# Wider descriptors for thirteen zero fills, and a short-DMA ending for the last one, in a decode-attention backward kernel

## The chip, the cores and the metric

One core of one Trainium2 chip. The metric is device time in microseconds (us) of one execution. Most executions of a kernel agree within 0.3%. An execution more than 1.5% above the fastest of the same kernel is called slow; verdicts use the other, fast, runs alone. "SyncE" is the engine that issues most DMAs here, "ACT" the scalar engine and "POOL" the engine whose DMAs go through the software queue. All three feed the same 16 DMA engines. A descriptor is one contiguous piece of a transfer that one engine moves; the trace records it as a packet. A semaphore is a counter that an instruction can wait for: in the traces each of the 16 engines raises it once when its part of a large DMA has landed, and that is called an increment below.

## The reference

A forward pass and its gradients: LayerNorm, an attention over the last 4,096 of 32,768 cached positions, a squared-ReLU MLP as a gate. What matters here is the shape of two of its ten outputs.

```python
# B=2, Hkv=8, Sk=32768, Dh=128, W=4096, all bfloat16
k = k_cache[:, :, Sk - W:, :]          # only the last W positions are used
v = v_cache[:, :, Sk - W:, :]
...
_out, _vjp = jax.vjp(_f, A_x, A_k_cache, A_v_cache, A_wq, A_wo, B_w1, B_b1, B_w2, B_b2)
```

The gradients of both caches (out_2 and out_3) have the caches' full size. Only 4,096 positions of each head can be other than zero. The other 28,672 positions, 7.34 MB for each of 32 (batch, head) parts, 235 MB in all, are zeros that the kernel has to write.

## The kernel before

POOL issues the zero fills of 31 of the 32 parts. The source is a tile of zero bytes that is widened to bfloat16 by the DMA, so a row of 14,336 source bytes becomes a descriptor of 28,672 bytes. Five parts (2, 4, 6, 8, 10) are cut in odd ways; these are not touched by the change.

```python
ZR = SK - W                     # 28672 rows of 256 B
ZG = 112
zt = const.tile([P, ZG * DH], mybir.dt.uint8, name="zt")
nc.vector.memset(zt[:].bitcast(F32), 0.0)

def zf(o, q, r0, nent, rows, rep=1):
    b, hk = divmod(q, HKV)
    nr = nent * rows * rep
    v = o[b, hk, r0:r0 + nr, :].rearrange("(r p g) d -> p r (g d)", p=nent, g=rows)
    st = 4 if nent < 16 else 1
    zs = zt[0:nent * st:st, 0:rows * DH].unsqueeze(1).to_broadcast([nent, rep, rows * DH])
    sw_fill.append(nc.gpsimd.dma_start(out=v, in_=zs))
    return r0 + nr
...
for qi in range(ZQ - 1):
    r = 0
    for n, rows, rep in zshort.get(qi, ((P, ZG, ZR // (P * ZG)),)):
        r = zf(*zparts[qi], r, n, rows, rep)
```

The compute chain runs beside the fills. It loads blocks of K and V (4.19 MB each), and stores their gradients. At its end SyncE stores dw2 and dw1, then issues the zeros of the 32nd part as one DMA of 512 descriptors of 14,336 B. This DMA is held back until the last fill but one has landed. ACT stores dwo last.

```python
last = nc.sync.dma_start(out=out_6.rearrange("(p k) f -> p k f", k=DK), in_=dw1_st[:])
b, hk = divmod(zparts[ZQ - 1][1], HKV)
v = out_3[b, hk, 0:ZR, :].rearrange("(r p g) d -> p r (g d)", p=P, g=ZG // 2)
zs = zt[:].bitcast(BF16).unsqueeze(1).to_broadcast([P, 2 * ZR // (P * ZG), ZG * DH // 2])
with tc.issue_after(last.ins):
    fin = nc.sync.dma_start(out=v, in_=zs)
tc.add_manual_dep(fin.ins, sw_fill[-2].ins.name, ...)
for j in range(NJ):
    ...                          # dwo, 32 matmuls and copies
dma_store.dma_start(out=out_5.rearrange("(p j) m -> p j m", j=NJ), in_=wo[:])
```

## Time and profile before

The median was 769.4 us over 6 runs (769.01 to 769.58).

| Reading | Value |
|---|---|
| span of the profiled run | 767.3 us |
| bytes moved, mean rate | 326.72 MB, 426 GB/s |
| dw2, dw1 issued | 701.4, 708.4 us |
| zeros of part 32 issued (SyncE) | 715.9 us |
| last packet of the POOL fills ends | 749.7 us |
| store of dwo issued, last data | 723.2, 748.7 us |
| last zeros of the 16 engines | 761.11 to 765.15 us |
| SyncE passes its wait for them | 765.49 us |

The ends of packets come from their records in the trace. The page of the kernel before, first its span, then the row of DMA busyness in 40 slices (9 means 90% or more), the rate in the same slices, and the queues (packets, MB, share of the 16 engines):

```profile
span 767.3 us, 9390 instructions
...
DMA  9999999999999999999999999999999999999997
GB/s 359 429 432 421 434 430 426 431 431 436 426 425 433 433 428 428 435 426 433 436 425 433 430 434 426 434 433 432 427 436 430 426 427 438 429 430 425 434 427 321
DMA packets 14202, 326.72 MB, mean 426 GB/s; under 512 B 2341, under 2 KB 2350, under 8 KB 2360
...
q0 software_dynamic: 9728, 227.55, 70.2%
q1 hardware_dynamic: 2698, 56.63, 17.8%
q10 hardware_dynamic: 1736, 41.95, 12.9%
```

The DMA engines are full from the first slice to the last but one, so the kernel can only become faster if the bytes move faster, or if the start or the end is used better. The busy shares of the other engines (PE 53%) don't matter here.

The time line of SyncE's issues after 700 us (start, duration, line, what is issued):

```profile
701.39 0.35 SPq L603 DMA_DIRECT2D out_dram<-dw_st  x1
708.37 0.35 SPq L611 DMA_DIRECT2D out_dram<-dw_st  x1
715.88 0.39 SPq L616 DMA_DIRECT2D out_dram<-zt  x1
```

POOL's waits (in total, how often, the longest):

```profile
POOL out_dram L96 <- DMA out_dram<-zt: 529.6, 30, 36.9
```

POOL waits 30 times for an earlier fill before it issues the next one. The operands of its DMAs show why: eight semaphores are used in rotation, and the issue of a DMA waits until the DMA that had its semaphore before has landed on all engines. SyncE and ACT share another eight in the same way.

The end of the kernel before, in windows. The last two columns are the busy share of the DMA engines and their rate:

```profile
core 0: us, PE busy (x) PEld busy (x) DVE busy (x) ACT busy (x) POOL busy (x), PEclk, DMA share, GB/s
758.00:761.00 3.00, 0.00 (x0) 0.00 (x0) 0.00 (x0) 0.00 (x0) 0.00 (x0) 0.50 1.03 440
...
762.00:763.00 1.00, 0.00 (x0) 0.00 (x0) 0.00 (x0) 0.00 (x0) 0.00 (x0) 0.50 0.37 158
...
764.00:765.00 1.00, 0.00 (x0) 0.00 (x0) 0.00 (x0) 0.00 (x0) 0.00 (x0) 0.50 0.07 29
...
766.00:767.00 1.00, 0.00 (x0) 0.00 (x0) 0.00 (x0) 0.00 (x0) 0.00 (x0) 0.50 0.00 0
```

From 761 us on the engines run out of work one by one: 0.07 of 16 engines is one engine. That one ends about 1 us after all the others.

### The profile page before, as it was taken

Reading aid. Unit: us, or ns where it says so; the run is one execution under the profiler, and the core shown is the slowest. Engines: PE = TensorE matmul, PEld = TensorE weight load, DVE = VectorE, ACT = ScalarE, POOL = GpSimd, SP = SyncE. Lnnn points to the kernel's source line nnn. Section 1 sums busy time; section 2 is a strip of 40 time slices with the busy share of each in tenths; the row PEclk is TensorE's granted clock in tenths of the full one; section 3 lists DMA queues with packets and bytes.
Section 4 is the critical chain, followed back from the end, with each engine's and each line's share of the span. In section 5 each row is a group of like instructions: output and inputs, shape, how many; then the busy total and the mean of one; then the engine's idle time right before and its main releaser. Section 6 shows DMA issues by size and latency. Waiting matters only on the chain.

```text
span 767.3 us, 9390 instructions
## 1 busy us (share of the span) xinstructions
PE 409.0 (53%) x4110; PEld 267.9 (35%) x4118; DVE 277.1 (36%) x484; ACT 214.8 (28%) x313; POOL 31.9 (4%) x55
## 2 busy tenths in 40 slices
PE   0166765847503757770385667304748853768600
PEld 0153464734103655430254543004635421342200
DVE  3034252455401346450152465302337541247500
ACT  0034441245500234560020255300244542004400
POOL 3000110110000010000000000000000000000000
PEclk9998898967755995775567958756986875655555
DMA  9999999999999999999999999999999999999997
GB/s 359 429 432 421 434 430 426 431 431 436 426 425 433 433 428 428 435 426 433 436 425 433 430 434 426 434 433 432 427 436 430 426 427 438 429 430 425 434 427 321
DMA packets 14202, 326.72 MB, mean 426 GB/s; under 512 B 2341, under 2 KB 2350, under 8 KB 2360
## 3 DMA queue, kind: packets, MB, share of 16 engines
q0 software_dynamic: 9728, 227.55, 70.2%
q1 hardware_dynamic: 2698, 56.63, 17.8%
q10 hardware_dynamic: 1736, 41.95, 12.9%
q8 instruction: 32, 0.52, 0.2%
q14 instruction: 8, 0.07, 0.0%
HBM read 45.62 MB, written 280.50 MB: 425 GB/s over the span
## 4 chain that ended last, share of the span: by engine, by line
DMA 36%; PE 32%; DVE 15%; ACT 8%; issue 4%; ACTq 0%; DVEq 0%; SPq 0%
DMA out_dram<-nat 15%; DMA nat<-in_A_k_cache_dram 9%; DMA nat<-in_A_v_cache_dram 8%; PE ov L403 6%; PE s_ps L376 4%; PE tp L370 4%; DMA b_bf<-in_B_b_dram 4%; DVE tT L149 3%; PE dp_ps L376 3%; DVE ds_bf L450 2%; ACT p_bf L437 2%; DVE nat L149 2%; PE wps L621 2%; ACT tT L147 2%; ACT nat L147 1%
## 5 line engine op out<-in xcount | busy, mean ns | idle before, releaser
L370 PE MATMUL tp<-pperm,nat 128*128 128x128 bf16 x1024 | 84.1, 233 | 129.0 <-DMA nat<-in_A_v_cache_dram 111.0
L149 DVE COPY tT<-tp 128x1024 bf16<-128x1024 bf16 x96 | 64.0, 688 | 202.5 <-PE tp L370 201.9
L370 PEld LDWEIGHTS <-nat 128*128 128x128 bf16 x1024 | 73.5, 105 | 135.3 <-DMA nat<-in_A_v_cache_dram 112.7
L147 ACT COPY tT<-tp 128x1024 bf16<-128x1024 bf16 x32 | 32.4, 1012 | 258.0 <-PE tp L370 258.0
L147 ACT CAST nat<-ov 128x512 bf16<-128x512 f32 x160 | 87.8, 589 | 54.0 <-PE ov L403 27.5
L149 DVE CAST nat<-ov 128x512 bf16<-128x512 f32 x96 | 65.3, 690 | 49.3 <-PE ov L403 48.1
L96 POOL DMA_DIRECT2D out_dram<-zt x47 | 30.8, 659 | 532.8 <-DMA out_dram<-zt 529.6
L403 PE MATMUL ov<-bd,ds_bf 128*128 128x512 bf16 x124 | 48.7, 467 | 6.7 <-DVE nat L149 4.0
L403 PE MATMUL ov<-bd,p_bf 128*128 128x512 bf16 x124 | 47.4, 446 | 5.3 <-DVE nat L149 1.8
L376 PE MATMUL dp_ps<-tT,zdo 128*128 128x256 bf16 x256 | 42.0, 298 | 14.6 <-DVE tT L149 8.3
L376 PE MATMUL s_ps<-tT,zq 128*128 128x256 bf16 x256 | 39.4, 279 | 13.2 <-DVE tT L149 9.5
L376 PEld LDWEIGHTS <-zdo 128*128 128x128 bf16 x256 | 25.9, 105 | 23.3 <-issue 19.7
L392 PE MATMUL ps<-t,nat 128*128 128x16 bf16 x1024 | 28.5, 173 | 7.8 <-DVE bd L360 7.8
L392 PEld LDWEIGHTS <-nat 128*128 128x128 bf16 x1024 | 28.6, 103 | 11.0 <-issue 5.8
L376 PEld LDWEIGHTS <-zq 128*128 128x128 bf16 x256 | 24.7, 99 | 19.9 <-issue 17.6
L488 PE MATMUL wps<-dq_rows,xn_bf 2*128 2x512 bf16 x32 | 14.2, 515 | 23.6 <-ACT wq L147 18.3
L384 PE MATMUL tp<-ident_bf,p_bf 128*128 128x128 bf16 x64 | 7.5, 312 | 35.0 <-ACT p_bf L437 35.0
L437 ACT ACTIVATE p_bf<-e_sb,rl 32x512 bf16<-32x512 f32 x16 | 22.8, 1424 | 3.4 <-DVE rl L434 3.2
L149 DVE CAST wq<-wps 128x512 bf16<-128x512 f32 x16 | 11.0, 690 | 31.5 <-PE wps L488 31.1
L147 ACT CAST dw_st<-wps 128x512 bf16<-128x512 f32 x15 | 8.8, 585 | 47.7 <-PE wps L601 44.9
L450 DVE SCALAR_TENSOR_TENSOR ds_bf<-dp_ps,delta,p_bf 32x512 bf16<-32x512 f32 x16 | 21.7, 1354 | 0.2
L403 PEld LDWEIGHTS <-ds_bf 128*128 128x128 bf16 x128 | 13.3, 111 | 23.1 <-issue 20.7
(196 smaller groups left out, 452.5 us busy)
## 6 DMA issues: line engine op xcount, KB each, us to landing
out_dram<-zt POOLq DMA_DIRECT2D x26, 7168.0 KB, 163.5
out_dram<-nat ACTq DMA_DIRECT2D x8, 4096.0 KB, 26.6
nat<-in_A_v_cache_dram SPq DMA_DIRECT2D x4, 4096.0 KB, 31.0
nat<-in_A_k_cache_dram SPq DMA_DIRECT2D x4, 4096.0 KB, 25.9
out_dram<-zt POOLq DMA_DIRECT2D x4, 3584.0 KB, 56.4
out_dram<-zt SPq DMA_DIRECT2D x1, 7168.0 KB
out_dram<-zt POOLq DMA_DIRECT2D x1, 5040.0 KB, 83.3
wo<-in_A_wo_dram SPq DMA_DIRECT2D x1, 4096.0 KB, 38.2
```

Of the source, the lines that this page charges most:

```text
L96: sw_fill.append(nc.gpsimd.dma_start(out=v, in_=zs))
L147: nc.scalar.copy(out=out_ap, in_=in_ap)
L149: nc.vector.tensor_copy(out=out_ap, in_=in_ap)
L370: nc.tensor.transpose(tp[:, j, :], nat[:, g * CC + half * CH + j, :], pperm[:].rearrange("p b k -> p (b k)"))
L376: nc.tensor.matmul(out_ps[:, half * CH * PB:(half + 1) * CH * PB], lhsT=zbuf[:, pr, o:o + R], rhs=tT[:, :, pr, :], start=(g == 0 and pr == ...
L384: nc.tensor.transpose(tp[:, cc, :], src[:, half * CH + cc].rearrange("r k b -> r (k b)"), ident_bf[:, :])
L392: nc.tensor.matmul(ps[:], lhsT=nat[:, g * CC + half * CH + cc, :], rhs=cols[half][:, cc, :, g, :], start=(half == 0 and g == 0 and cc == 0 ...
L403: nc.tensor.matmul(ov[:], lhsT=src[:, cc].rearrange("r k b -> r (k b)"), rhs=bd[:, gh * 4:(gh + 1) * 4, :], start=True, stop=True)
L437: nc.scalar.activation(out=p_bf[rb, :, :, pr], in_=e_sb[rb], func=ACT.Copy, scale=rl[rb, 0:1])
L450: nc.vector.scalar_tensor_tensor(out=ds_bf[rb, :, :, pr], in0=dp_c[rb], scalar=delta[rb, 0:1], in1=p_bf[rb, :, :, pr], op0=ALU.subtract, o ...
L488: nc.tensor.matmul(wps[:], lhsT=xn_bf[:, k:D:DK], rhs=dq_rows[:, :], start=True, stop=True)
L621: nc.tensor.matmul(wps[:], lhsT=o_rows[:, j:N:NJ], rhs=ds_rows[:, :], start=True, stop=True)
```

## The change

Its intent is to halve the number of descriptors where the fills have the engines to themselves (source bytes widened to 4-byte elements, 57,344 B for each descriptor), and to give the engines different amounts at the very end, so that they finish together. Of the zeros of part 32, 384 rows go into eight short DMAs over the first 2, 4, 6 to 14 and then 8 engines.

```diff
@@ def zf
-        v = o[b, hk, r0:r0 + nr, :].rearrange("(r p g) d -> p r (g d)", p=nent, g=rows)
+        v = o[b, hk, r0:r0 + nr, :]
+        w = rows * DH
+        if w > ZG * DH:
+            v = v.bitcast(F32)
+            w //= 2
+        v = v.rearrange("(r p g) d -> p r (g d)", p=nent, g=rows)
         st = 4 if nent < 16 else 1
-        zs = zt[0:nent * st:st, 0:rows * DH].unsqueeze(1).to_broadcast([nent, rep, rows * DH])
+        zs = zt[0:nent * st:st, 0:w].unsqueeze(1).to_broadcast([nent, rep, w])
@@
+    zlong = (3, 5, 7, 11, 12, 16, 17, 18, 19, 22, 23, 24, 28)
@@
-        for n, rows, rep in zshort.get(qi, ((P, ZG, ZR // (P * ZG)),)):
+        whole = (P, ZR // P, 1) if qi in zlong else (P, ZG, ZR // (P * ZG))
+        for n, rows, rep in zshort.get(qi, (whole,)):
@@ the end
-    v = out_3[b, hk, 0:ZR, :].rearrange("(r p g) d -> p r (g d)", p=P, g=ZG // 2)
-    zs = zt[:].bitcast(BF16).unsqueeze(1).to_broadcast([P, 2 * ZR // (P * ZG), ZG * DH // 2])
-    with tc.issue_after(last.ins):
-        fin = nc.sync.dma_start(out=v, in_=zs)
-    tc.add_manual_dep(fin.ins, sw_fill[-2].ins.name,
-                      mybir.DependencyInfo(mybir.DependencyClass.Sync, mybir.DependencyReason.DATA))
+    zb = zt[:].bitcast(BF16)
+    r = 0
+    for n, g, rep, st in ((P, 56, 3, 1), (P, 53, 1, 1), (2, 1, 1, 8), (4, 2, 1, 8), (6, 3, 1, 8), (8, 4, 1, 8), (10, 5, 1, 8), (12, 6, 1, 8),
+                          (14, 7, 1, 8), (8, 13, 1, 8)):
+        v = out_3[b, hk, r:r + n * g * rep, :].rearrange("(r p g) d -> p r (g d)", p=n, g=g)
+        zs = zb[0:n * st:st, 0:g * DH].unsqueeze(1).to_broadcast([n, rep, g * DH])
+        with tc.issue_after(last.ins):
+            fin = nc.sync.dma_start(out=v, in_=zs)
+        if r == 0:
+            tc.add_manual_dep(fin.ins, sw_fill[-2].ins.name,
+                              mybir.DependencyInfo(mybir.DependencyClass.Sync, mybir.DependencyReason.DATA))
+        last = fin
+        r += n * g * rep
+    assert r == ZR
```

## The prediction

> **What bounds the kernel now.** The DMA engines. The page gives 326.72 MB at a mean of 426 GB/s over a span of 767.3 us, and the slice row shows DMA at 9 tenths or more in all slices but the last (PE 53%). The Trainium skill ("DMA: Bandwidth & Descriptors", Where 436 GB/s comes from) puts the ceiling at 435.2 GB/s; stretches with fills alone (280 to 300 us) move 431.2 GB/s in the trace, so 1% is left there. The compute chain is not the limit: in the timeline its last copy ends at 723.1 us, the store of dwo has landed by 750.6, and the zeros issued by SyncE run alone until 765.15. In that tail the 16 engines' last zeros land between 761.11 and 765.15 (mean 762.7); 2.2 us of closing waits follow.
>
> **56 KB descriptors.** The thirteen fills are those that run almost alone on the engines (16.2 or more busy with that queue), about 17.1 us each. A 28,672-byte packet starts every 1,057 ns (median) behind the previous one; 32 B at a time at the skill's rate would be 1,054. So joining two packets saves some 3 ns: 13 fills x 8 packets fewer per engine x 3 ns is about 0.3 us (estimate). One engine differs: in 406 to 452 and 546 to 594 us one chain of packets averages 1,098 ns against 1,057. If its 41 ns are paid per descriptor it gains about 4 us, but others then end last: the second latest ends 1.07 us before the latest, worth at most about 1 us. Where a load meets a 56 KB fill it gets a smaller share of the engine; the chain has some 30 us of slack, so this costs nothing.
>
> **Short ending.** The 128-partition part shrinks by 24 rows per engine, 6,144 B or 0.23 us. Engines 0 and 1 get 41 rows instead, 14 and 15 none: a redistribution of about 0.2 to 0.5 us. Against it stands a new wait. The DMAs of SyncE and ACT use eight semaphores in rotation, and the issues wait for a semaphore's previous DMA (POOL's fills wait so for 529.6 us). Ten DMAs on eight: the seventh waits for dw1 (landed 739.5 in before), the eighth for dwo (750.6), both harmless; the ninth waits until the first 24-packet part has landed on all engines, the tenth until the second part has. After the slowest engine's last 13.5 KB packet about 0.33 us pass until SyncE goes on (765.15 to 765.49 in before), then an issue of 0.35 us and about 1 us from issue to first packet (0.74 to 1.7 us at the start). So the last small DMA runs alone at the end: about +1 us.
>
> **Sum.** -0.3 (packets), -0.5 (slow engine, half believed), -0.2 (shrunk part), +1.1 (late issues): 769.4 becomes 769.5 us. Range 767.9 to 771.0. Chances: faster by over 2% 0.01, within 2% 0.97, slower by over 2% 0.02.
>
> **What would show it.** Packets of 57,344 B at about 2,110 ns apart; DMA GB/s of those slices up by less than 1%; SyncE's last issues after 761 and after 764 us, waiting for zeros.
>
> **What would make it wrong.** Widening bytes to four-byte elements may run below the write rate (packets well above 2,130 ns): each 5% costs 11 us. The slow engine may have set more of the end than I think, giving 2 us. The semaphores may be dealt out otherwise: no late issues.

## The result

The kernel after took 770.54 us (median of 10 runs). Eight of them lie between 770.20 and 770.72; two were slow, at 802.67 and 804.16 us. The kernel before took 769.21 us beside it (median of 20, 768.92 to 769.76). The ratio is 1.0016, with a 95% interval of 1.0007 to 1.0026. Ratios are the mean time of one kernel's fast runs over that of the other's in the same rounds, so they aren't quite the ratio of the medians that are quoted. The 1.3 us are clear of noise, and so are the two slow runs, of which more below.

The page of the kernel after, in the lines shown of before:

```profile
span 768.6 us, 9399 instructions
...
DMA  9999999999999999999999999999999999999996
GB/s 356 432 431 422 450 413 431 439 430 420 430 434 431 428 440 431 420 429 434 429 436 441 431 431 420 433 431 430 442 428 431 425 431 429 450 421 420 429 427 287
DMA packets 12682, 326.72 MB, mean 425 GB/s; under 512 B 2423, under 2 KB 2486, under 8 KB 2504
...
q0 software_dynamic: 8064, 227.55, 70.0%
q1 hardware_dynamic: 2842, 56.63, 17.9%
q10 hardware_dynamic: 1736, 41.95, 13.1%
```

The software queue has 1,664 packets fewer (13 x 128), as intended, for the same bytes. The last slice went from 321 to 287 GB/s: the loss is at the end.

SyncE's issues of the last part, in several windows of its time line (the first five issues follow each other from 714.26 us and are left out):

```profile
727.25 0.61 SPq L627 DMA_DIRECT2D out_dram<-zt  x1
...
743.23 0.75 SPq L627 DMA_DIRECT2D out_dram<-zt  x1
...
750.20 0.76 SPq L627 DMA_DIRECT2D out_dram<-zt  x1
...
760.81 0.78 SPq L627 DMA_DIRECT2D out_dram<-zt  x1
...
764.92 0.61 SPq L627 DMA_DIRECT2D out_dram<-zt  x1
```

And its waits after 700 us:

```profile
SPq L627 <- DMA out_dram<-dw_st: 25.1, 2, 15.4
...
SPq L627 <- DMA out_dram<-zt: 13.1, 2, 9.8
...
SPq L627 <- DMA out_dram<-wo: 6.2, 1, 6.2
```

Each late issue waits for the previous user of its semaphore. The sixth waits for dw2, the seventh for dw1, the eighth for dwo. The ninth waits 9.8 us for the first large part of the ending to land on all engines, the tenth 3.3 us for the second. The windows at the end:

```profile
758.00:761.00 3.00, 0.00 (x0) 0.00 (x0) 0.00 (x0) 0.00 (x0) 0.00 (x0) 0.50 1.00 425
...
762.00:763.00 1.00, 0.00 (x0) 0.00 (x0) 0.00 (x0) 0.00 (x0) 0.00 (x0) 0.50 0.39 153
...
764.00:765.00 1.00, 0.00 (x0) 0.00 (x0) 0.00 (x0) 0.00 (x0) 0.00 (x0) 0.50 0.02 6
765.00:766.00 1.00, 0.00 (x0) 0.00 (x0) 0.00 (x0) 0.00 (x0) 0.00 (x0) 0.50 0.00 0
766.00:767.00 1.00, 0.00 (x0) 0.00 (x0) 0.00 (x0) 0.00 (x0) 0.00 (x0) 0.50 0.10 27
```

From 765 to 766 us the engines are idle; from 766 on the last eight packets, of 3,328 B, run alone. The trace's records of packets and of semaphore increments give this chain for the end:

| Event | before, us | after, us |
|---|---|---|
| last packet of the large part(s) ends on the slowest engine | 765.15 | 764.42 |
| last semaphore increment for it | 765.47 | 764.90 |
| SyncE issues the tenth DMA | – | 764.92 |
| its first packet starts | – | 766.17 |
| its last increment | – | 766.78 |
| SyncE passes the wait | 765.49 | 766.80 |

So the main work of the slowest engine was done 0.57 us earlier than in before (765.47 - 764.90), and the late tenth DMA gave back 1.88 us (766.78 - 764.90).

**Which engine ends last** can be read from the short packets, although the records don't name engines. The Trainium skill ("DMA: Bandwidth & Descriptors", Why a DMA increments its semaphore by 16 and not by 1) says that a DMA over k engines from this kind of queue runs on the lowest-numbered k. The trace agrees as far as it goes: each short size occurs on as many engines as the DMA has partitions, and the sets are nested. On the slowest engine the first short packet, at 764.42 us, is one of 768 B. It has no 256 B or 512 B packet, so it is by this rule the fifth or sixth engine (number 4 or 5). The next engine was done with its large parts 0.9 us earlier. Experiment 2 below shows the same pair, again with a 768 B packet first on the engine that ends last.

### The profile page after: what moved, and what is told of

It reads as the page before. It is cut to its first block, busy times and chain, and to the rows that moved or that the text cites. A ratio compares the mean times of both kernels' runs of the same rounds, so it can differ in the third digit from the quotient of the medians.

```text
span 768.6 us, 9399 instructions
## 1 busy us (share of the span) xinstructions
PE 408.9 (53%) x4110; PEld 267.8 (35%) x4118; DVE 277.1 (36%) x484; ACT 214.8 (28%) x313; POOL 29.8 (4%) x55
## 4 chain that ended last, share of the span: by engine, by line
PE 35%; DMA 31%; DVE 15%; ACT 9%; issue 4%; ACTq 0%; DVEq 0%; SPq 0%
DMA out_dram<-nat 12%; DMA nat<-in_A_v_cache_dram 8%; DMA nat<-in_A_k_cache_dram 7%; PE ov L410 6%; PE tp L377 5%; PE s_ps L383 4%; DMA b_bf<-in_B_b_dram 4%; DVE tT L156 3%; PE dp_ps L383 3%; DVE ds_bf L457 2%; ACT p_bf L444 2%; DVE nat L156 2%; PE wps L636 2%; ACT nat L154 2%; ACT tT L154 2%
## 5 line engine op out<-in xcount | busy, mean ns | idle before, releaser
L101 POOL DMA_DIRECT2D out_dram<-zt x47 | 28.7, 613 | 533.6 <-DMA out_dram<-zt 530.3
L399 PE MATMUL ps<-t,nat 128*128 128x16 bf16 x1024 | 28.5, 173 | 7.8 <-DVE bd L367 7.8
L383 PEld LDWEIGHTS <-zq 128*128 128x128 bf16 x256 | 24.8, 100 | 19.2 <-issue 16.8
```

Source lines behind the costliest of these rows:

```text
L383: nc.tensor.matmul(out_ps[:, half * CH * PB:(half + 1) * CH * PB], lhsT=zbuf[:, pr, o:o + R], rhs=tT[:, :, pr, :], start=(g == 0 and pr == ...
L399: nc.tensor.matmul(ps[:], lhsT=nat[:, g * CC + half * CH + cc, :], rhs=cols[half][:, cc, :, g, :], start=(half == 0 and g == 0 and cc == 0 ...
```

## The experiments

Four kernels were run together each time, with the kernel before on the same chip: its median was 769.4 us for experiments 1 to 4, 769.28 for 5 to 8, and 769.21 for 9 to 12. My theory (A) was that the loss comes from the last two short DMAs, whose issue waits for a semaphore. The rivals were that wide fills cost something (B), and that short DMAs cost something by themselves, whatever the order (C).

### 1. The wide fills alone

```diff
-    for n, g, rep, st in ((P, 56, 3, 1), (P, 53, 1, 1), (2, 1, 1, 8), ...
+    # ending of the kernel before: one SyncE DMA of 512 descriptors
```

> The thirteen 56 KB fills alone, with the ending of before. Theory A (the loss of after comes from the two last short DMAs, whose issue waits for their semaphore): 768.5 to 769.0 us, ratio 0.9990 to 1.0000, SyncE's end wait passed 0.3 to 0.7 us earlier than in before. Rival B (wide fills unbalance the engines or cost the loads, and that is the loss): 770.3 us or more. If the two slow runs of after (802.7 and 804.2 us) come from the wide descriptors, about 2 of 10 runs here are slow too.

Measured: 768.94 us (5 runs, 768.55 to 769.35, none slow), ratio 0.9995, interval 0.9981 to 1.0008. By the medians that is 0.46 us below before; the interval includes a ratio of 1, so it may be none. B fails for the fast runs. The expected earlier end doesn't show in the trace: in the profiled run (the longest of the five, 769.35 us) the last increment landed at 765.70 us, against 765.47 in before. And five runs without a slow one are too few to say that wide fills alone have none.

### 2. The ending alone

```diff
-    zlong = (3, 5, 7, 11, 12, 16, 17, 18, 19, 22, 23, 24, 28)
+    # all whole fills with 28 KB descriptors, zf as in the kernel before
```

> The short ending alone, with all fills at 28 KB. Theory A: 770.7 to 771.1 us, 1.5 to 1.9 us over before; SyncE issues its ninth and tenth DMA of the ending at about 761 and 765 us, and 3,328 B packets run alone at the end. Rival B: within 0.3 us of before.

Measured: 771.08 us (770.79 to 771.34), ratio 1.0022, interval 1.0010 to 1.0035. That is 1.68 us over before. The two parts add up: -0.46 + 1.68 = 1.22 us, and the whole change cost 1.33. SyncE's time line in this run shows the same two late issues; this answer merges them into a line that starts at 761.57 us and spans 4.71 us:

```profile
761.57 4.71 SPq L620 DMA_DIRECT2D out_dram<-zt  x2
```

### 3. The two smallest first

```diff
-    ((P, 56, 3, 1), (P, 53, 1, 1), (2, 1, 1, 8), (4, 2, 1, 8), (6, 3, 1, 8), ...
+    ((2, 1, 1, 8), (4, 2, 1, 8), (P, 56, 3, 1), (P, 53, 1, 1), (6, 3, 1, 8), ...
```

> The kernel after with the same ten SyncE DMAs, the two smallest moved to the front: the ninth and tenth now wait for these two, which land before 745 us, and not for the two large parts. Theory A: 768.5 to 769.1 us, 1.5 to 2 us below after; no issue of SyncE after 755 us. Rival C (short DMAs cost by themselves, by their number, descriptors or write receipts, whatever the order): stays at 770.3 to 770.7.

Measured: 769.94 us (769.73 to 770.33), ratio to before 1.0009, interval 0.9996 to 1.0021. That is 0.60 us below after, not 1.5 to 2. Neither A nor C gave this number, and the trace shows two things that I hadn't counted on.

First, the compute chain was late in this run: dwo was issued at 743.3 us, against 723.2 in before and 728.6 in after. The eighth DMA waits for dwo's semaphore, so SyncE stood for 22.6 us there, and the last three issues came at 761.8 to 763.4 us. So my "no issue after 755 us" was wrong. The line of waits:

```profile
SPq L627 <- DMA out_dram<-wo: 22.6, 1, 22.6
```

Second, on the slowest engine the increments of the short DMAs come one after the other long after their packets. Second large part: 765.04 us; the six short DMAs behind it: 765.24, 765.43, 765.62, 765.81, 765.99 and 766.18. They are 0.19 us apart, while the packets themselves were all done by 764.96. In after five such increments run from 765.09 to 765.84, hidden by the later wait. The skill (same page, Queues, rings and completion order) says that an increment lands only after every earlier write of that engine. A queue of increments behind slow write receipts would look like this; the trace shows the spacing, not its cause.

### 4. All 26 whole fills wide

```diff
-        whole = (P, ZR // P, 1) if qi in zlong else (P, ZG, ZR // (P * ZG))
+        whole = (P, ZR // P, 1) if qi not in zshort else (P, ZG, ZR // (P * ZG))
```

The ending is that of before.

> All 26 whole fills with 56 KB descriptors, ending of before. If the worth of a joined packet is 3 ns and the chain's slack is about 30 us: 768.3 to 768.9 us although the loads beside fills get a smaller share of the engines and the last store of the compute chain is issued 5 to 25 us later than 723 us. If the slack is smaller than the delay, the store of dwo lands last and the time rises above 770 us.

Measured: 820.73 us (4 runs, 817.96 to 820.96), ratio 1.066. This is the second of the two cases that I had named, but far larger than I expected. The windows of this run:

```profile
680.00:700.00 20.00, 16.31 (x219) 8.87 (x217) 11.29 (x18) 12.41 (x24) 0.00 (x0) 0.83 0.98 415
700.00:720.00 20.00, 14.46 (x91) 6.70 (x92) 10.80 (x18) 10.72 (x18) 0.00 (x0) 0.79 0.79 340
720.00:740.00 20.00, 17.00 (x111) 8.54 (x110) 3.94 (x8) 4.13 (x6) 0.00 (x0) 0.61 0.49 211
740.00:760.00 20.00, 11.12 (x150) 8.88 (x149) 8.21 (x26) 0.00 (x0) 0.00 (x0) 0.56 0.01 2
```

The fills were done at 697.8 us, 52 us earlier than in before (749.7), and dwo was issued at 799.5 us, 76 us later. In between the engines ran dry. The reason is the share that each queue gets. From 380 to 398 us, with one load, one store and a wide fill in flight, the software queue moved 201.6 GB/s and the other two 116.2 and 115.1: a ratio of 1.73, where 57,344 to 32,768 B is 1.75. In before, from 350 to 370 us, the same three shared as 136, 154 and 142. So the engines give each queue one packet in turn. The records of before show the turns: from 354.4 us on, 16 packets of SyncE's queue start one after another, then 16 of ACT's (355.6 to 356.6), then POOL's again, one packet for each engine. A wider packet takes time away from the loads that the compute chain waits for. A wide fill alone on the engines takes it from nobody; that is how the thirteen had been chosen.

### 5. The short ones first

```diff
-    ((P, 56, 3, 1), (P, 53, 1, 1), (2, 1, 1, 8), (4, 2, 1, 8), (6, 3, 1, 8), (8, 4, 1, 8), (10, 5, 1, 8), ..., (8, 13, 1, 8))
+    ((6, 3, 1, 8), (8, 4, 1, 8), (10, 6, 1, 8), (12, 6, 1, 8), (14, 7, 1, 8), (8, 13, 1, 8), (P, 56, 3, 1), (P, 53, 1, 1))
```

> The kernel after with an ending of eight DMAs, as many as there are semaphores: six short ones first (374 of the 384 small rows kept, 10 more on the fifth), then the two large parts. Nothing small is left behind the large parts. From the third experiment's trace the increments of short DMAs that follow each other on the slowest engine land 0.19 us apart. If late issue (first) and these serial increments (second) are the whole cost of the ending: 768.8 to 769.2 us, about 1 us below the third experiment and about the same as the wide fills alone. If short DMAs cost by their number in any place: 769.7 us or more.

Measured: 770.30 us (769.89 to 771.27), ratio 1.0014, interval 1.0002 to 1.0026. This fits the rival's number, but the trace has another reason. The chain was late again (dwo issued at 742.4 us), and now a large part stood behind dwo's semaphore:

```profile
SPq L627 <- DMA out_dram<-wo: 22.5, 1, 22.5
```

Its windows show the engines half idle in the middle of the ending, before the second large part arrives:

```profile
761.00:762.00 1.00, 0.00 (x0) 0.00 (x0) 0.00 (x0) 0.00 (x0) 0.00 (x0) 0.50 1.09 459
762.00:763.00 1.00, 0.00 (x0) 0.00 (x0) 0.00 (x0) 0.00 (x0) 0.00 (x0) 0.50 0.52 217
763.00:764.00 1.00, 0.00 (x0) 0.00 (x0) 0.00 (x0) 0.00 (x0) 0.00 (x0) 0.50 1.03 434
```

I had moved the wait, not removed it. Experiment 9 repeats the test without this flaw.

### 6. Narrow fills

```diff
-        whole = (P, ZR // P, 1) if qi in zlong else (P, ZG, ZR // (P * ZG))
+        whole = (P, ZG // 2, 2 * ZR // (P * ZG)) if qi in zlong else (P, ZG, ZR // (P * ZG))
```

The same thirteen fills with 14 KB descriptors, the ending of before.

> The same thirteen fills with 14 KB descriptors, ending of before: twice as many packets as in before in these fills, four times as many as in after. If a packet costs 4.4 ns (0.46 us measured for 104 packets fewer per engine): 208 packets more, +0.9 us, 770.1 to 770.5 us. If width matters for another reason than the number of packets (contiguity in HBM, say): within 0.3 us of before, 769.1 to 769.7.

Measured: 769.60 us (769.50 to 769.78), ratio 1.0005, interval 0.9993 to 1.0017: 0.32 us over before, a third of what I expected, and not clear of noise. The time from one packet's start to the next on an engine orders the three widths: in stretches with fills alone (564 to 592 us) its median is 530 ns at 14 KB, 1,057 at 28 KB and 2,111 at 56 KB in after, so 2,120, 2,114 and 2,111 ns for the same 57,344 B. Joining two packets saves some 3 ns in either step, so each doubling of the width is worth half of the one before. (The rates over these 28 us, 429.9, 431.7 and 432.0 GB/s, can't tell 28 KB from 56: other runs with 28 KB fills, experiments 2 and 9, have 431.5 and 430.7.)

### 7. The kernel after again

No edit.

> The kernel after, unchanged, for its slow runs: 770.3 to 770.8 us in fast runs. If the 802 and 804 us belong to this kernel, 0 to 3 of 6 runs are 30 us longer again; if they were chance of that chip, none is.

Measured: five fast runs from 770.49 to 771.25 us (two of them above the expected 770.8) and two slow ones, 788.35 and 803.52; the 788.35 us were the profiled run. So the slow runs belong to the kernel: 4 of 18 executions of it over the two comparisons (profiled ones counted), and none of the 31 of the kernel before beside them. The windows of the slow one:

```profile
700.00:720.00 20.00, 12.98 (x161) 8.92 (x158) 6.64 (x19) 0.00 (x0) 0.00 (x0) 0.66 1.02 431
720.00:740.00 20.00, 11.86 (x51) 5.42 (x51) 14.40 (x17) 3.52 (x6) 0.00 (x0) 0.50 0.35 136
740.00:760.00 20.00, 19.19 (x45) 6.13 (x45) 13.81 (x22) 12.66 (x22) 0.00 (x0) 0.50 0.76 320
```

This is experiment 4 in small. The fills ended at 728.9 us, dw2 and dw1 were issued at 741.7 and 748.7, and the engines were mostly idle between. The records of packets show where the delay arose:

| Transfer, us from first to last packet | before | after, fast | after, slow |
|---|---|---|---|
| second-last cache load (V) | 500.2 to 525.1 | 495.2 to 519.8 | 505.7 to 530.7 |
| last cache load (K) | 526.3 to 544.5 (18.2) | 524.0 to 543.4 (19.4) | 534.2 to 562.7 (28.5) |
| last store of a cache gradient | 624.1 to 642.8 (18.7) | 631.0 to 650.2 (19.2) | 657.1 to 683.2 (26.1) |

In the fast run of after the last load ends at 543.4 us, when wide fill 22 begins: its first packet starts at 541.7 us, and most engines begin it after 544. In the slow run the chain was 10 us later by then, fill 22 began at 531.8, and the load met it for its whole length. That delayed the next steps into wide fill 28 (from 654.2 us). In this run a small delay was enlarged by each wide fill that it ran into. All of this lies before the ending is issued (749 us), and experiment 8 has the ending of before and is late in every run, so the new ending isn't needed for it.

### 8. Three more wide fills

```diff
-    zlong = (3, 5, 7, 11, 12, 16, 17, 18, 19, 22, 23, 24, 28)
+    zlong = (3, 5, 7, 11, 12, 14, 20, 21, 16, 17, 18, 19, 22, 23, 24, 28)
```

The ending is that of before; fills 14, 20 and 21 ran beside loads and stores there.

> Wide fills 14, 20 and 21 too, which run beside loads and stores, ending of before. In the run with all 26 wide the fills ended at 698 us and the two dw stores were issued at 778 and 785 us, so the engines ran dry. If the delay of the chain is about proportional to the number of wide fills beside transfers (76 us for 13): dw1 is issued 10 to 25 us later than in before, the fills end a little earlier, and the time is still 768.5 to 769.2. If the slack is used up already with three, over 775 us, with some idle DMA slices after 700 us.

Measured: six runs from 787.54 to 801.59 us, ratio 1.0334 from the three that count as fast (787.54 to 799.18); the profiled one, 801.59 us, counts as slow. The slack is used up with three. dwo was issued at 780.5 us, 57 us later than in before, and the engines stood almost idle from 740 to 760 us:

```profile
740.00:760.00 20.00, 12.73 (x49) 4.74 (x48) 15.46 (x14) 5.08 (x9) 0.00 (x0) 0.50 0.03 12
```

The delay isn't proportional to the number of wide fills (76 us for thirteen more); my expectation from proportion failed. The times are those of the slow runs of after, now in every run.

### 9. Six DMAs on 28 KB fills

```diff
 # fills and the rest as in experiment 2
-    ((P, 56, 3, 1), (P, 53, 1, 1), (2, 1, 1, 8), ..., (14, 7, 1, 8), (8, 13, 1, 8))
+    ((8, 13, 1, 8), (10, 11, 1, 8), (12, 6, 1, 8), (14, 7, 1, 8), (P, 56, 3, 1), (P, 53, 1, 1))
```

> All fills at 28 KB as in before, so that the compute chain is not late; the ending as six DMAs, four short ones first (about the same rows per engine: 37 on the lowest engines, none on the last two), then the two large parts. No issue of the ending waits for dwo or for another DMA of the ending. If late issue and serial increments are the cost of the ending, it is gone: 769.1 to 769.6 us, 1.5 us or more below the ending of after on the same fills (771.1). If the redistribution itself or the number of short DMAs cost: 770 us or more.

Measured: 769.30 us (768.95 to 769.82), ratio 1.0001, interval 0.9989 to 1.0014. The cost of the ending is gone: 771.08 became 769.30, each beside its own before of 769.4 and 769.21. All six issues follow each other within 4.4 us:

```profile
723.44 4.40 SPq L619 DMA_DIRECT2D out_dram<-zt  x6
```

With about the same rows on short DMAs in front (37 against 41 on the lowest engines), and no wait, they cost nothing that shows. For four short DMAs C, in the form "in any place", fails. After has eight: eight in front, all issued in time, weren't run.

### 10. The two smallest first, on 28 KB fills

```diff
 # fills and the rest as in experiment 2, the ten DMAs in the order of experiment 3
```

> All fills at 28 KB, the ten DMAs of after with the two smallest first. No issue after 755 us, so the wait for the large parts is gone, but six increments still follow the second large part on the slowest engine, 0.19 us each, 1.1 us in all. Expected 0.5 to 1.0 us over before (769.8 to 770.4) and about 1 us below the ending of after on the same fills. If late issue were everything: within 0.3 us of before.

Measured: 770.17 us (769.83 to 770.54), ratio 1.0012, interval 1.0000 to 1.0025: 0.96 us over before, at the edge of the noise. Experiment 2 was 1.68 us over its own before, so the late issue by itself is worth 0.72 us by the medians (the two sets of runs, 770.79 to 771.34 and 769.83 to 770.54, don't overlap). The last issue was at 741.8 us, so none is left behind the large parts. The ten issues, merged into one line:

```profile
722.93 19.49 SPq L620 DMA_DIRECT2D out_dram<-zt  x10
```

The last increment of the second large part on the slowest engine came at 765.13, and the six behind it at 765.33, 765.52, 765.72, 765.90, 766.09 and 766.27: 1.14 us in steps of 0.19. This is the part of C that holds: short DMAs behind the last large one cost their increments in series.

### 11. Six wide fills and a relieved engine

```diff
-    zlong = (3, 5, 7, 11, 12, 16, 17, 18, 19, 22, 23, 24, 28)
+    zlong = (11, 12, 17, 18, 23, 24)
-    ((P, 56, 3, 1), (P, 53, 1, 1), (2, 1, 1, 8), ..., (8, 13, 1, 8))
+    ((4, 32, 4, 8), (P, 55, 4, 1))
```

> Six wide fills only (11, 12, 17, 18, 23, 24), each in the middle of a stretch without transfers, and an ending of two DMAs: 32 KB more for each of the first four engines, 32 rows less for all. In the traces one of engines 4 and 5 ends last by 0.9 us or more in every run of the short ending. Expected: -0.2 (wide) -0.3 (the late engine relieved): 768.6 to 769.1 us, dw1 issued within 6 us of before, no slow run.

Measured: 768.77 us (768.66 to 769.23, none slow), ratio 0.9995, interval 0.9982 to 1.0007. SyncE passed its last wait at 765.09 us, against 765.49 in before. It is the lowest median of all kernels here, 0.44 us below before, but the interval includes a ratio of 1. Five runs are also too few to say that six wide fills have no slow runs: after has 4 in 18, and experiment 1, with all thirteen, had none in five. The sentence on "every run of the short ending" doesn't hold for experiment 5: there the last packets of all 16 engines ended within 0.2 us of each other.

### 12. The relieved engine alone

```diff
 # as experiment 11, all whole fills with 28 KB descriptors
```

> The ending of the run beside this one on 28 KB fills: what that ending is worth alone. Expected 768.9 to 769.3 us, 0 to 0.4 us below before. If the engine that ends last is among the first four (the reading of the short packets is wrong): 0.5 us or more over before.

Measured: 768.83 us (768.69 to 769.32), ratio 0.9996, interval 0.9982 to 1.0010. That is within 0.1 us of experiment 11, so six wide fills add nothing that can be measured. Had the late engine been one of the first four, this ending would have made it about 1 us later (96 rows of 256 B more); it didn't, which supports the reading that it is number 4 or 5.

## Why the prediction was right or wrong

The time, 770.54 us, lies inside the range of 767.9 to 771.0, 1.0 us above the stated 769.5. The wait that the prediction named is the one that the trace shows, but the stated sum, +0.1 us, was too low: a gain of 0.5 us never came, and the end cost 0.8 us more than thought, mostly for a reason that the prediction didn't have. The range was wide enough to hold both. Point by point:

- **"What bounds the kernel now. The DMA engines."** Right: dw1 was issued anywhere between 697.6 and 728.5 us in fast runs whose medians lie within 2.3 us of each other, and most of these 2.3 us go back to the endings.
- **"So joining two packets saves some 3 ns ... about 0.3 us."** Right in size. Packets of 57,344 B follow each other at 2,111 ns (median) in the fill-only stretches of after, against 2 x 1,057: 3 ns. Experiment 1 gave -0.46 us by its medians.
- **"One engine differs ... If its 41 ns are paid per descriptor it gains about 4 us"**, entered as -0.5 ("half believed"). Wrong. In after the slow chain of packets averages 2,201 ns against 2,113 from 406 to 452 us: 88 ns for each 57,344 B, where it was 41 for 28,672 B. The loss goes with the bytes, not with the descriptors, so nothing was to be had. The skill (same page, Latency and other measured facts) puts a usual slowness of two engines, 7 and 15, down to the traffic of fetching descriptors, as a guess. If that were the cause here, half the descriptors should have lowered the loss for the same bytes, and they didn't (88 ns against 2 x 41). But which engine this chain is on isn't known.
- **"the ninth waits until the first 24-packet part has landed on all engines, the tenth until the second part has."** Right, to a fraction of a microsecond: issues at 760.81 and 764.92, where "after 761" and "after 764" were forecast. Experiment 10 takes these two waits away on the same fills, and of 1.68 us over before 0.96 are left. Experiment 9 takes away the short DMAs behind the large parts as well, and 0.09 are left.
- **"+1.1 (late issues)"** was the other mis-sized term of the sum. It measured 1.88: 0.02 us from the increment to the issue, 1.25 from the issue to the first packet, 0.26 for the packets and 0.35 to the last increment. I had counted the issue and about 1 us, and forgotten that the tenth DMA has its own wait for its increment at the end, although I had named its size. But not all of the 1.88 us is owed to the lateness. Had the tenth been issued in time, the six short DMAs would still have landed one after the other behind the large part, as in experiment 10: 6 x 0.19 = 1.14 us. The lateness itself is the other 0.74 us, and the medians of experiments 2 and 10 say the same (1.68 - 0.96 = 0.72). So the late issue cost less than the +1.1 stated, and the larger part of the cost was the serial increments, which the prediction didn't have.
- **"-0.2 (shrunk part)"**: the slowest engine's last large increment was 0.57 us earlier than in before; the shrunk part and the wide packets together predict 0.5. That fit may be luck: the same end came at 765.24 us in experiment 2 (shrunk part alone) and at 765.36 in experiment 1 (wide packets alone), both later than the 765.15 of before. The redistribution also went the wrong way for the engine that ends last. If it is number 4 or 5, it lost 24 rows of the large part and got 3 + 4 + 5 + 6 + 7 + 13 = 38 rows in short DMAs.
- **"the chain has some 30 us of slack, so this costs nothing"**: right for the fast runs only. dwo was issued 40, 57 and 76 us later than in before in the profiled runs of experiments 7, 8 and 4, and these were 19, 32 and 51 us longer than that of before (769.10 us). So the slack was 21 to 25 us, somewhat less than stated, and the delay isn't bounded: in one slow run a wide fill stretched a load from about 19 to 28.5 us, and the chain ended 35 us later than in a fast one. The prediction gave the slow runs no chance at all.

With the terms as measured or worked out the sum is -0.46 (wide) - 0.23 (shrunk part) + 1.88 (late issue) = +1.2 us, against 1.33 measured. Of these only the last is read from the trace of after; the first rests on medians whose interval includes zero, and the second is worked out from the rows.

**What stays open:** why the increments are 0.19 us apart; what starts the delay in a slow run (dw1 was issued between 697.6 and 718.5 us in fast runs with all fills at 28 KB too); whether eight short DMAs in front of the large parts, issued in time, cost anything; whether the slow runs near 803 us, which weren't profiled, are the same thing as the 788 us one that was; and the worth of wide fills more exactly than "0 to 1 us".

## What to carry to other kernels

Where DMAs draw their semaphores from a small rotation, count the DMAs of an ending: one too many waits for a large one issued just before it, and its round trip then stands alone at the end (here 1.9 us, 0.7 us more than without the wait). Put short pieces in front of the last large transfer, not behind it: here four in front cost nothing that shows, and the increments of six behind it took 1.1 us. A wider descriptor is a larger share of every engine on which another queue also has work, so widen fills only where nothing that the compute chain waits for can meet them, with a margin for a late chain; the gain is a few ns for each packet and the risk is tens of us.

## What the Trainium skill lacked or had wrong

- "DMA: Bandwidth & Descriptors", Queues, rings and completion order: it says that an engine drains a packet of typically 9 to 17 descriptors from one queue before it switches. With descriptors of 28 to 56 KB the turns here are single descriptors: in before each queue in turn starts 16 packets, one for each engine (354.4 to 356.8 us), and in experiment 4 the three queues shared as 201.6, 116.2 and 115.1 GB/s with 57,344, 32,768 and 32,768 B. That a larger descriptor then takes its share from other queues isn't said.
- The same page, Anatomy of one DMA (about the software queue's path, while the short DMAs here are SyncE's): it calls the bubble of a semaphore write tiny, about one cycle. The 4-byte packets of the increments here are short too, 9 ns each. What the page lacks is the spacing of the landings: the increments of short DMAs behind each other on one engine landed 0.19 us apart, six in a row, though their packets were done.
- The same page, Latency and other measured facts: the usual slowness of engines 7 and 15 is put down, as a guess, to descriptor fetches. Here one engine lost 41 ns for 28 KB and 88 ns for 56 KB, so with the bytes. The records don't name this engine, so this isn't a test of the page; the engine that ends last is read as 4 or 5.
- No page has the cost of reusing a semaphore that is still in flight: here an issue waited up to 22.6 us for one in a fast run (experiment 3).
